# Splitting the last accumulator and its store, and holding one block's late products, in a two-layer attention and MLP kernel

## The chip, the cores and the metric

One core of one Trainium2 chip. The metric is device time in microseconds (us), the median of several executions. All executions compared here ran at a granted TensorE clock of 0.999 to 1.0. The experiments ran on two chips (e3, e4, e7 and e8 on one, the others on the other), so each median is set against runs of the kernel before in the same rounds.

## The reference

```python
# S = 2048 tokens, D = 1024, F = 3584, bfloat16; two identical rounds:
x = x + A(layernorm(x))   # sliding local attention: qkv, 8 taps at distance 2, softmax, output projection
x = x + B(layernorm(x))   # gate, up, relu(gate) * up, then W_down back to D columns
x = x + A(layernorm(x))
x = x + B(layernorm(x))
return x                  # 2048 x 1024, bfloat16
```

## The kernel before

The tokens are cut into 4 blocks of 512 (4 tiles of 128 rows each), and two rounds of 4 blocks make 8 steps, n = 0 to 7; below, "block 2" is the block of step 2, and so on. The steps are interleaved so that TensorE always has matmuls while VectorE does the attention of a later block. The residual x stays in SBUF in 16 tiles of 128x1024. Three parts matter.

The down projection of step n, and the store of a finished block:

```python
def down_steps(n, hold):
    ...
    def f_(half, s8):                      # half: 512 of the 1024 output columns; s8: a slab of 8 row blocks of W_down
        def f():
            if s8 == 0:
                accs[half] = [psum.tile([P, BLK], F32, tag="acc", ...)[:] for t in range(TPB)]   # 4 of 6 buffers
            ...
            for t in range(TPB):           # 4 token tiles
                with pe_group():
                    for jl in range(nfc):
                        mm(ac[t], lhsT=hT[:, j, t * P:(t + 1) * P], rhs=wsl[:, jl, :], ...)      # 128x512
            if s8 == NSL - 1:
                for t in range(TPB):
                    xs = xt[:, half * SLAB:(half + 1) * SLAB]
                    nc.vector.tensor_tensor(xs, ac[t], xs, op=ALU.add)     # "x add": PSUM + residual
        ...
    return [f_(half, s8) for half in range(2) for s8 in range(NSL)]

def store_x(n):                            # after the last step of a block: four stores of 128x1024
    for t in ...: sp_dma(out_dram[t * P:(t + 1) * P, :], x_tiles[t][:])
```

The attention logits of blocks 1 to 7 are sums of products on VectorE. A step makes the product `t` of head chunk c and then adds the previous one into `ac` (two halves h, 8 chunks each):

```python
def mult(h, c):
    def f():
        ...
        nc.vector.tensor_tensor(t[:], i0, i1, op=ALU.mult)     # n == 1: inside tc.issue_after(gate[0])
        if c > 1: add(h, c - 1)
        if c == KC - 1: add(h, c)

def add(h, c):
    nc.vector.tensor_tensor(o, ac[:], t[:], op=ALU.add)        # 128x2048, f32
```

VectorE's instruction order is made by a scheduler from the program; `tc.issue_after(ins)` adds an ordering edge, so that what is built inside it comes after `ins` on the same engine. `sp_dma` issues a DMA from the SP queue, always behind the DMA issued there before it. In the names of the profile, `dacc` is the accumulator of the down projection, `x` the residual, `t` and `ac` the products and their sum.

Of the kernel before, what the change touches and what calls it, by code (L numbers as in the profile page):

```python
# [8 lines left out]
F32 = mybir.dt.float32  # L9
ALU = mybir.AluOpType  # L10
# [3 lines left out]
P = 128  # L14
# [7 lines left out]
BLK = 512  # L22
TPB = BLK // P
EPS = 1e-5
NEG = -1.0e9
SLAB = 512
# [10 lines left out]
def kernel(  # L37
# [11 lines left out]
    nc = tc.nc  # L49
# [3 lines left out]
    NB = S // BLK  # L53
# [7 lines left out]
    NN = PAIRS * NB  # L61

    x_dram = A_x.flatten_outer_dims()
    out_dram = out.flatten_outer_dims()
# [16 lines left out]
    psum = ctx.enter_context(tc.tile_pool(name="psum", bufs=6, space=bass.MemoryType.PSUM))  # L81
# [28 lines left out]
    gate = [None]  # L110

    def sp_dma(dst, src, transpose=False):
        start = nc.sync.dma_start_transpose if transpose else nc.sync.dma_start
        if tail_sp[0] is None:
            tail_sp[0] = start(dst, src).ins
        else:
            with tc.issue_after(tail_sp[0]):
                tail_sp[0] = start(dst, src).ins

    @contextmanager  # L120
    def pe_group():
        if tail_pe[0] is None:
            yield
        else:
            with tc.issue_after(tail_pe[0]):
                yield

    def mm(*args, **kwargs):
        tail_pe[0] = nc.tensor.matmul(*args, **kwargs).ins  # L129

    def big_tile(shape, name, early=False):
        where = pool["early"] if early else big
        return where.tile(shape, BF16, tag="big", name=name)
# [27 lines left out]
    for t in range(NT):  # L161
        xt = xpool.tile([P, D], BF16, name=f"x{t}")
# [328 lines left out]
    def red_mm(n, prod, first, last):  # L491
        st = att[n]
        if first:
            st["L"] = psum_l.tile([P, W, P], F32, tag="L", name=f"L_{n}")
        with pe_group():
            for wh in range(2):
                for tq in range(TPB):
                    mm(st["L"][32 * tq:32 * tq + 32, WH * wh:WH * (wh + 1), :], lhsT=sel[:],
                       rhs=prod[:, WH * wh:WH * (wh + 1), tq * P:(tq + 1) * P],
                       start=first, stop=last, skip_group_check=True, tile_position=(0, 32 * tq))  # L500

    def qk_bcast(n, c, w0, nw):
        q, k = att[n][("q", c)], att[n][("k", c)]
        return _ap(q, 0, [[0, nw], [1, BLK]]), _ap(k, HALO - DIL * w0, [[-DIL, nw], [1, BLK]])
# [18 lines left out]
    def prod_sum_steps(n):  # L523
        st = att[n]

        def mult(h, c):
            def f():
                if h == 0 and c == 0:
                    st["s"] = big_tile([P, W, BLK], f"s_{n}")
                i0, i1 = qk_bcast(n, c, WH * h, WH)  # L530
                if c == 0:
                    t = work.tile([P, WH, BLK], F32, tag="ac", name=f"ac_{n}_{h}", bufs=1)
                    st["ac"] = t
                else:
                    t = work.tile([P, WH, BLK], F32, tag="t", name=f"t_{n}_{h}_{c}")
                    st[("t", c)] = t
                if n == 1:
                    with tc.issue_after(gate[0]):
                        nc.vector.tensor_tensor(t[:], i0, i1, op=ALU.mult)
                else:  # L540
                    nc.vector.tensor_tensor(t[:], i0, i1, op=ALU.mult)  # L541
                if c > 1:
                    add(h, c - 1)
                if c == KC - 1:
                    add(h, c)
            return f

        def add(h, c):
            ac, t = st["ac"], st.pop(("t", c))
            o = st["s"][:, WH * h:WH * (h + 1), :] if c == KC - 1 else ac[:]  # L550
            nc.vector.tensor_tensor(o, ac[:], t[:], op=ALU.add)  # L551

        def red():
            red_mm(n, st["s"], True, True)

        return [mult(h, c) for h in range(2) for c in range(KC)], red
# [97 lines left out]
    def gu_steps(n, ln):  # L654
        hold = {}

        def f_(j):
            def f():
                if j == 0:
                    hold["hT"] = pool["hid"].tile([P, FC, BLK], BF16, tag="hT", name=f"hT_{n}")  # L660
                s4, jl = j // 4, j % 4
                accs = {}
                for nm in ("g", "u"):
                    acc = psum.tile([P, BLK], F32, tag="acc", name=f"acc_{nm}")
                    with pe_group():
                        for kc in range(KC):
                            mm(acc[:], lhsT=slab[(nm, n, s4)][:, kc, jl * P:(jl + 1) * P], rhs=ln["xnT"][:, :, kc, :],
                               start=(kc == 0), stop=(kc == KC - 1))
                    accs[nm] = acc
                    if nm == "g":  # L670
                        r = pool["hid"].tile([P, BLK], BF16, tag="r", name="r", bufs=3)
                        tail_act[0] = nc.scalar.activation(r[:], acc[:], ACT.Relu).ins  # L672
                nc.vector.tensor_tensor(hold["hT"][:, j, :], accs["u"][:], r[:], op=ALU.mult)  # L673
            return f

        return [f_(j) for j in range(FC)], hold

    def down_steps(n, hold):
        b = n % NB
        accs = {}  # L680

        def f_(half, s8):
            def f():
                hT = hold["hT"]
                if s8 == 0:
                    accs[half] = [psum.tile([P, BLK], F32, tag="acc", name=f"dacc{t}")[:] for t in range(TPB)]
                ac = accs[half]
                nfc = min(8, FC - 8 * s8)
                wsl = slab[("d", n, half, s8)]
                for t in range(TPB):  # L690
                    with pe_group():
                        for jl in range(nfc):
                            j = 8 * s8 + jl
                            mm(ac[t], lhsT=hT[:, j, t * P:(t + 1) * P], rhs=wsl[:, jl, :],
                               start=(j == 0), stop=(j == FC - 1))
                if s8 == NSL - 1:
                    for t in range(TPB):
                        xt = x_tiles[b * TPB + t]
                        xs = xt[:, half * SLAB:(half + 1) * SLAB]
                        nc.vector.tensor_tensor(xs, ac[t], xs, op=ALU.add)  # L700
            return f

        return [f_(half, s8) for half in range(2) for s8 in range(NSL)]
# [106 lines left out]
    for n in range(NN):  # L810
        gu, hold = gu_steps(n, ln_b[n])
        want_gu(n, at, 2 * GRP)
        spread(gu, at, 2 * GRP)
        if n == 0:
            spread(pv_steps(1), at + 66.0, 5.5)
            ev.append((at + 105.0, store_o(1)))
            ev.append((at + 105.1, load_o(1)))
        elif n + 1 < NN:
            ev.append((at + 0.1, reds_n[n + 1]))
            ev.append((at + 0.2, lambda n=n: softmax(n + 1)))  # L820
            spread(pv_steps(n + 1), at + 12.0, 6.5)
            ev.append((at + 72.0, store_o(n + 1)))
            ev.append((at + 72.1, load_o(n + 1)))
        if n + 2 < NN:
            ln1(n + 2, at + 30.0, at + 58.0)
        at += 2 * GRP * FC
        if n + 2 < NN:
            want_qk(("qk", n + 2), at + 2 * GRP * KC)
            spread(qk_steps(n + 2, ln_a[n + 2], ("qk", n + 2)), at, GRP)
            sums, reds_n[n + 2] = prod_sum_steps(n + 2)  # L830
            spread(sums, at + GRP * (K_STEP[0] + 1.0), 4.4)
            at += 2 * GRP * KC
            if n + 2 >= NB:
                want_v(("v", n + 2), at + GRP * KC / 2, at + GRP * KC)
                spread(v_steps(n + 2, ln_a[n + 2], ("v", n + 2)), at, GRP)
                at += GRP * KC
                ev.append((at + 3.0, store_v(n + 2)))
        if n + 1 < NN:
            want_wo(n + 1, at + GRP * TPB, at + 2 * GRP * TPB)
            spread(wo_steps(n + 1), at, 2 * GRP)  # L840
            ln2(n + 1, [at + GRP * TPB + GRP * (t + 1) + 0.1 for t in range(TPB)], at + 2 * GRP * TPB + 31.0)
            at += 2 * GRP * TPB
        if n + 2 < NN:
            spread(load_v_steps(n + 2), at + 4.0, 6.5)
        want_down(n, at, GRP / 2)
        spread(down_steps(n, hold), at, 4 * GRP)
        at += GRP * FC
        if n >= NN - NB:
            ev.append((at + 4.0, store_x(n)))
    slab_events(ev)  # L850
    emit(ev)
# [32 lines left out]
```

## Time and profile before

| | before |
|---|---|
| median of 3 runs (range) | 1630.64 us (1630.27 to 1630.65) |
| span of the profiled run | 1628.4 us |
| TensorE (PE) busy | 1618.6 us, 99% |
| one wait of PE for VectorE (DVE) near 308 us | 0.76 us |
| last matmul's end to the end of the span | 3.90 us |

The page, first the busy line of each engine, then the chain that ended last as shares of the span:

```profile
span 1628.4 us, 18703 instructions
...
PE 1618.6 (99%) x7589; PEld 782.2 (48%) x7638; DVE 1062.6 (65%) x926; ACT 506.1 (31%) x1050; POOL 255.7 (16%) x220
...
PE 95%; DVE 4%; issue 1%; DMA 0%; POOL 0%; DVEq 0%
```

PE is the bound. The waits of PE (who waited for whom: us in total, times, longest) say what it ever waits for:

```profile
engine line waited for: us in total, times, longest us
PE scratch L129 <- DVE ones L296: 1.5, 1, 1.5
PE dacc L129 <- DVE x L700: 0.8, 1, 0.8
PE acc_v L129 <- DVE xnT_first L103: 0.6, 1, 0.6
PE tp L364 <- DVE xn_first L103: 0.4, 1, 0.4
```

All but the second are start-up. The second is in block 0's down projection. The timeline of PE there (start, length, what, and in brackets the idle time before it and what ended it):

```profile
299.65 7.72 PE L129 MATMUL dacc<-w_d,hT 128*128 128x512 bf16 x35
308.13 1.24 PE L129 MATMUL dacc<-w_d,hT 128*128 128x512 bf16 x5 [0.76 <-DVE x L700]
```

and that of DVE:

```profile
300.66 2.29 DVE L541 TENSOR_TENSOR t<-q,k 128x2048 f32<-128x2048 bf16 x1
302.87 2.28 DVE L551 TENSOR_TENSOR ac<-ac,t 128x2048 f32<-128x2048 f32 x1
305.18 2.29 DVE L541 TENSOR_TENSOR t<-q,k 128x2048 f32<-128x2048 bf16 x1
307.39 2.47 DVE L700 TENSOR_TENSOR x<-dacc,x 128x512 bf16<-128x512 f32 x4
309.79 2.28 DVE L551 TENSOR_TENSOR ac<-ac,t 128x2048 f32<-128x2048 f32 x1
```

The four accumulators of half 0 were complete near 303.9 us (estimate: PE ran dry at 307.37, 16 matmuls of 0.216 us later), but DVE was in the middle of its sums and came to the x adds only at 307.39. PE used the two free accumulators for half 1 and then had to wait for the first add.

The end of the kernel, in the timeline:

```profile
1595.81 28.65 PE L129 MATMUL dacc<-w_d,hT 128*128 128x512 bf16 x129
...
1622.63 2.92 SPq L118 DMA_DIRECT2D out_dram<-x  x4
...
1624.50 0.69 DVE L700 TENSOR_TENSOR x<-dacc,x 128x512 bf16<-128x512 f32 x1 [0.17 <-PE dacc L129]
1625.22 0.33 SPq L118 DMA_DIRECT2D out_dram<-x  x1
```

(The last line is the fourth of the four merged issues, from a narrower window.) The last matmul ends at 1595.81 + 28.65 = 1624.46, the last add at 1625.19, its store is issued at 1625.22, and the span ends at 1628.37. The table of stretches gives the traffic in that time; the last two columns are the busy share of the DMA engines and GB/s:

```profile
1625.20:1626.00 0.80, 0.00 (x0) 0.00 (x0) 0.00 (x0) 0.00 (x0) 0.00 (x0) 1.00 0.88 325
1626.00:1627.00 1.00, 0.00 (x0) 0.00 (x0) 0.00 (x0) 0.00 (x0) 0.00 (x0) 1.00 0.70 262
1627.00:1628.40 1.40, 0.00 (x0) 0.00 (x0) 0.00 (x0) 0.00 (x0) 0.00 (x0) 0.99 0.00 0
```

The DMA engines are nearly full until the data ends (at 1626.89 by the packets), then 1.48 us pass without data. From the DMA issues we can split them. The last figure of this line is the time from the issue of the last store to its landing (us), when its semaphore has all its increments:

```profile
out_dram<-x SPq DMA_DIRECT2D x1, 256.0 KB, 2.0
```

The landing comes 0.37 us after the last data, and the program then takes 1.10 us to end.

### The profile page before, as it was taken

How to read it: one execution, taken by the hardware profiler on the slowest of the kernel's cores; microseconds unless marked ns; L12 is line 12 of the kernel's file. 1: busy time of each engine (PE TensorE's matmuls, PEld its weight loads, DVE VectorE, ACT ScalarE, POOL GpSimd, SP SyncE). 2: the span in 40 equal slices, each digit the busy share in tenths (PEclk: the TensorE clock that was granted, in tenths of full speed). 3: DMA queues.
4: the chain of work that ended last, by engine and by line, in shares of the span. 5: the costliest groups of instructions: out<-in, count | busy, mean ns of one | idle time of the engine just before them, and what ended most of it. 6: DMA issues, size and time to landing. Idle time of an engine off the chain costs nothing.

```text
span 1628.4 us, 18703 instructions
## 1 busy us (share of the span) xinstructions
PE 1618.6 (99%) x7589; PEld 782.2 (48%) x7638; DVE 1062.6 (65%) x926; ACT 506.1 (31%) x1050; POOL 255.7 (16%) x220
## 2 busy tenths in 40 slices
PE   9999999999999999999999999999999999999999
PEld 6644445444544445444454444544445444444444
DVE  5799899985497927949179492894818958211211
ACT  4754313243241513405134051331513311131110
POOL 2421003310250102201052010520105100000000
PEclk9999999999999999999999999999999999999999
DMA  9579656746476485664857647577484764655451
GB/s 303 93 203 252 167 177 199 192 156 200 136 215 175 155 233 171 184 175 150 229 181 185 187 150 225 162 203 212 151 231 154 194 205 155 206 164 172 156 168 65
DMA packets 371463, 296.83 MB, mean 182 GB/s; under 512 B 142512, under 2 KB 351664, under 8 KB 370480
## 3 DMA queue, kind: packets, MB, share of 16 engines
q1 hardware_dynamic: 371088, 295.23, 63.2%
q8 instruction: 60, 0.98, 0.3%
q10 hardware_dynamic: 288, 0.39, 0.1%
q14 instruction: 27, 0.22, 0.0%
HBM read 256.77 MB, written 21.00 MB: 171 GB/s over the span
## 4 chain that ended last, share of the span: by engine, by line
PE 95%; DVE 4%; issue 1%; DMA 0%; POOL 0%; DVEq 0%
PE acc_g L129 24%; PE acc_u L129 24%; PE dacc L129 22%; PE acc_v L129 7%; PE acc_k L129 6%; PE acc_q L129 6%; PE acc_wo L129 6%; DVE t L541 2%; DVE ac L551 1%; PE L L129 1%; DVE pv L603 0%; DVE x L648 0%; DVE pv L604 0%; DVE ac L541 0%; DMA x<-in_A_x_dram 0%
## 5 line engine op out<-in xcount | busy, mean ns | idle before, releaser
L129 PE MATMUL acc_g<-xnT_b,w_g 128*128 128x512 bf16 x1792 | 423.4, 379 | 0.0
L129 PE MATMUL acc_u<-xnT_b,w_u 128*128 128x512 bf16 x1792 | 423.3, 379 | 0.0
L129 PE MATMUL dacc<-w_d,hT 128*128 128x512 bf16 x1759 | 386.5, 379 | 2.5 <-DVE x L700 0.8
L672 ACT ACTIVATE r<-acc_g 128x512 bf16<-128x512 f32 x224 | 133.4, 596 | 747.1 <-PE acc_g L129 746.0
L673 DVE TENSOR_TENSOR hT<-acc_u,r 128x512 bf16<-128x512 f32 x224 | 153.7, 687 | 315.1 <-PE acc_u L129 313.5
L129 PEld LDWEIGHTS <-hT 128*128 128x128 bf16 x1792 | 175.4, 98 | 212.3 <-issue 1.0
L129 PEld LDWEIGHTS <-w_g 128*128 128x128 bf16 x1792 | 174.8, 98 | 212.7 <-issue 3.0
L129 PEld LDWEIGHTS <-w_u 128*128 128x128 bf16 x1792 | 175.4, 98 | 211.4
L541 DVE TENSOR_TENSOR t<-q,k 128x2048 f32<-128x2048 bf16 x84 | 191.7, 2290 | 8.6 <-ACT k L480 5.8
L551 DVE TENSOR_TENSOR ac<-ac,t 128x2048 f32<-128x2048 f32 x84 | 191.7, 2282 | 0.4
L485 POOL COPY kh<-k 128x14 bf16<-128x14 bf16 x64 | 81.2, 1273 | 471.9 <-ACT k L480 471.8
L700 DVE TENSOR_TENSOR x<-dacc,x 128x512 bf16<-128x512 f32 x64 | 42.5, 687 | 164.0 <-PE dacc L129 164.0
L603 DVE TENSOR_TENSOR pv<-a,vhm 128x4096 bf16<-128x4096 bf16 x64 | 145.2, 2282 | 0.0
L129 PE MATMUL acc_wo<-w_o,oT 128*128 128x512 bf16 x496 | 111.0, 379 | 0.8
L245 POOL TENSOR_TENSOR st_b<-st_b,neg_half 128x1 f32<-128x1 f32 x29 | 56.4, 1956 | 288.6 <-ACT st_b L244 288.6
L245 POOL TENSOR_TENSOR st_a<-st_a,neg_half 128x1 f32<-128x1 f32 x32 | 41.9, 1315 | 319.2 <-ACT st_a L244 319.1
L484 POOL COPY k<-kh 128x14 bf16<-128x14 bf16 x48 | 70.5, 1469 | 65.9 <-DVE t L541 43.8
L129 PEld LDWEIGHTS <-oT 128*128 128x128 bf16 x512 | 50.0, 98 | 60.4
L604 DVE TENSOR_TENSOR pv<-pv 128x2048 bf16<-128x2048 bf16 x64 | 77.4, 1215 | 0.2
L476 ACT CAST q<-acc_q 128x512 bf16<-128x512 f32 x64 | 37.3, 583 | 73.2 <-PE acc_q L129 73.2
L240 ACT ACTIVATE xn_b<-x 128x1024 bf16<-128x1024 bf16 x29 | 30.3, 1045 | 89.3 <-DVE x L648 89.3
L480 ACT CAST k<-acc_k 128x512 bf16<-128x512 f32 x64 | 37.3, 583 | 63.0 <-PE acc_k L129 62.8
(131 smaller groups left out, 1209.1 us busy)
## 6 DMA issues: line engine op xcount, KB each, us to landing
w_g<-in_B_W_gate_dram SPq DMA_DIRECT2D x56, 1024.0 KB, 7.0
w_u<-in_B_W_up_dram SPq DMA_DIRECT2D x56, 1024.0 KB, 5.4
w_d<-in_B_W_down_dram SPq DMA_DIRECT2D x48, 1024.0 KB, 5.8
w_o<-in_A_wo_dram SPq DMA_DIRECT2D x16, 1024.0 KB, 7.2
vhm<-v_d SPq DMA_DIRECT2D x32, 284.0 KB, 6.9
v_d<-vT SPq DMA_DIRECT2D x8, 1024.0 KB, 10.0
oT<-o_d SPq DMA_DIRECT2D x32, 256.0 KB, 4.4
w_d<-in_B_W_down_dram SPq DMA_DIRECT2D x16, 512.0 KB, 4.0
```

What stands on the lines that cost most here:

```text
L129: tail_pe[0] = nc.tensor.matmul(*args, **kwargs).ins
L245: nc.gpsimd.tensor_tensor(rstd, vpe, neg_half[:, 0:1], op=ALU.pow)
L476: tail_act[0] = nc.scalar.copy(q[:], acc[:]).ins
L484: nc.gpsimd.tensor_copy(k[:, 0:HALO], khalo[n - 1][:, c, :])
L485: nc.gpsimd.tensor_copy(khalo[n][:, c, :], k[:, BLK:BLK + HALO])
L541: nc.vector.tensor_tensor(t[:], i0, i1, op=ALU.mult)
L551: nc.vector.tensor_tensor(o, ac[:], t[:], op=ALU.add)
L603: nc.vector.tensor_tensor(tt[:], a_bc, v_sh, op=ALU.mult)
L604: nc.vector.tensor_tensor(tt[:, 0:4], tt[:, 0:4], tt[:, 4:8], op=ALU.add)
L672: tail_act[0] = nc.scalar.activation(r[:], acc[:], ACT.Relu).ins
L673: nc.vector.tensor_tensor(hold["hT"][:, j, :], accs["u"][:], r[:], op=ALU.mult)
L700: nc.vector.tensor_tensor(xs, ac[t], xs, op=ALU.add)
```

## The change

The intent is twofold. The end is shortened: block 7 is stored in half rows as soon as each half is added, and the last tile's second half ends as two accumulators of 256 columns with an add and a store each. And block 2's products that come late are held behind the x adds of block 0's first half, so that PE need not wait for those.

```diff
-                if n == 1:
-                    with tc.issue_after(gate[0]):
+                behind = gate[0] if n == 1 else down_gate[0] if n == 2 else None
+                if behind is not None:
+                    with tc.issue_after(behind):
                         nc.vector.tensor_tensor(t[:], i0, i1, op=ALU.mult)
                 else:
                     nc.vector.tensor_tensor(t[:], i0, i1, op=ALU.mult)
...
+    down_gate = [None]
...
+                cols = [(t, 0, SLAB) for t in range(TPB)]
+                if n == NN - 1 and half == 1:
+                    cols[-1:] = [(TPB - 1, 0, SLAB // 2), (TPB - 1, SLAB // 2, SLAB)]
                 if s8 == 0:
-                    accs[half] = [psum.tile([P, BLK], F32, tag="acc", name=f"dacc{t}")[:] for t in range(TPB)]
+                    accs[half] = [psum.tile([P, BLK], F32, tag="acc", name=f"dacc{t}") for t, _, _ in cols]
...
-                for t in range(TPB):
+                for a, (t, c0, c1) in zip(ac, cols):
...
-                            mm(ac[t], lhsT=hT[:, j, t * P:(t + 1) * P], rhs=wsl[:, jl, :],
+                            mm(a[:, c0:c1], lhsT=hT[:, j, t * P:(t + 1) * P], rhs=wsl[:, jl, c0:c1],
...
-                        xs = xt[:, half * SLAB:(half + 1) * SLAB]
-                        nc.vector.tensor_tensor(xs, ac[t], xs, op=ALU.add)
+                        xs = xt[:, half * SLAB + c0:half * SLAB + c1]
+                        ins = nc.vector.tensor_tensor(xs, a[:, c0:c1], xs, op=ALU.add).ins
+                        if n == 0 and half == 0:
+                            down_gate[0] = ins
+                        if n == NN - 1:
+                            row = (b * TPB + t) * P
+                            col = half * SLAB + c0
+                            sp_dma(out_dram[row:row + P, col:col + c1 - c0], xs)
...
-        if n >= NN - NB:
+        if NN - NB <= n < NN - 1:
             ev.append((at + 4.0, store_x(n)))
```

The diff does not tell what the scheduler makes of the hold. The built program does. On DVE around block 0's first half (t5 stands for the product of chunk 5, and so on):

```
before:  ... t4, ac+=t3, t5,      x add x4,  ac+=t4, t6, ac+=t5, ...
after:   ... t4, ac+=t3, ac+=t4,  x add x4,  t5,     t6, ac+=t5, ...
```

More of the change, by code (lines that the diff above doesn't have):

```diff
@@ L693, in f @@
                             j = 8 * s8 + jl
-                            mm(ac[t], lhsT=hT[:, j, t * P:(t + 1) * P], rhs=wsl[:, jl, :],
+                            mm(a[:, c0:c1], lhsT=hT[:, j, t * P:(t + 1) * P], rhs=wsl[:, jl, c0:c1],
                                start=(j == 0), stop=(j == FC - 1))
                 if s8 == NSL - 1:
-                    for t in range(TPB):
+                    for a, (t, c0, c1) in zip(ac, cols):
                         xt = x_tiles[b * TPB + t]
-                        xs = xt[:, half * SLAB:(half + 1) * SLAB]
-                        nc.vector.tensor_tensor(xs, ac[t], xs, op=ALU.add)
+                        xs = xt[:, half * SLAB + c0:half * SLAB + c1]
[6 more added lines that the diff above has]
+                            sp_dma(out_dram[row:row + P, col:col + c1 - c0], xs)
             return f
```

## The prediction

> **What bounds the kernel now.** TensorE. The page has PE busy 1618.6 of 1628.4 us at full clock; the chain that ended last is 95% PE. The waits view of PE lists 3.3 us: start-up, and one wait of dacc for DVE (x add), 0.8 us. Otherwise only the end is exposed. Last matmul ends about 1624.48, last x add 1624.50 to 1625.19, its 256 KB store is issued about 1625.2, data moves until about 1626.8, the span ends at 1628.4 (timeline, stretches). The change can touch about 0.8 + 3.9 us (0.3%).
>
> **Part 1: sums of block 2 behind the adds.** In the timeline of block 0's down projection, PE runs dry at 307.37 and resumes at 308.13. Half 0 ended about 303.9 (estimate: 16 matmuls at 0.2157 us filled the two free accumulators), but DVE, which the Trainium skill ("TensorE: Matmul & The Clock Gate", specifications table) calls strict FIFO, reached the x adds only at 307.39, behind products and accumulations: the trace agrees with FIFO. The intent is to bring the adds forward. But in the changed kernel's instruction order only product t5 moves behind them; the accumulation of t4 takes its place. Before: ac(t3), t5, x adds, ac(t4). After: ac(t3), ac(t4), x adds, t5. A product takes 2.29 us, an accumulation 2.28 (timeline): the adds start at 307.4 to 307.5 as before, and the PE gap stays 0.75 to 0.87 us. No gain, 0.05 lost.
>
> **Part 2: the end.**
> - PE: 28 matmuls of 512 columns become 56 of 256. In block 0's v projection 56 of 256 columns with 16 of 512 took 9.57 us (15.12 to 24.69): 0.109 us each (estimate) against 0.2157 for 512. 56 x 0.109 - 28 x 0.2157 = +0.07 us. Weight loads (98 ns) still fit beneath; five accumulators fit the six buffers.
> - Last add: 0.69 us at 512 columns, about 0.40 at 256 (estimate from 0.69 and 2.28 us at 2048: 0.15 + 0.00104 per column). It ends about 0.5 instead of 0.71 us after the last matmul: -0.2 us. SP takes about 0.33 us per issue, so the last store goes out about 0.55 after: no more than -0.2.
> - Last store: 64 KB instead of 256. Its data took about 0.75 us (8 packets of 2 KB per engine, about 85 ns each). The skill ("DMA: Bandwidth & Descriptors", specifications) gives 512 B as the smallest size at line rate, just met here. Packets of 1 KB took 46 ns, of 256 B 18 ns, so 8 of about 27 ns: 0.2 to 0.3 us (estimate), -0.45 us. The 0.8 us from issue to data and the 1.6 us from last data to end stay.
> - The half-0 stores move to about 1598.5 to 1602, where DMA is idle. The last w_d slab goes out behind them near 1601.4, not 1596.9; needed about 1621.
>
> **Sum.** +0.05 + 0.07 - 0.2 - 0.45 = about -0.5 us: 1630.1 us, range 1629.5 to 1630.9, 8 in 10. Faster by over 2%: 0.003; within 2%: 0.994; slower: 0.003.
>
> **What would show it.** PE still waits 0.75 to 0.9 us for DVE x near 308; the last add takes about 0.4 us and ends 0.5 after the last matmul; from there to the end of the span 2.8 instead of 3.2 us.
>
> **What would make it wrong.** DVE reaching the adds early after all (0.8 us more gained); slower 256-column matmuls; stores queueing on SP; run spread (0.4 us in three runs).

## The result and the profile after

| | before | after |
|---|---|---|
| median (range), 4 runs each | 1630.45 us (1630.27 to 1630.65) | 1629.69 us (1629.53 to 1630.22) |
| PE's wait in block 0 | 0.76 us | 0.77 us |
| first matmul of block 0's down projection to the last matmul's end | 1344.88 us | 1344.97 us |
| last matmul's end to the end of the span | 3.90 us | 3.37 us |

The ratio is 0.9996 (95% interval 0.9979 to 1.0013): the same within 2%, and a gain of 0.76 us in the medians. A ratio is the mean time of one kernel's fast runs over that of the other's of the same rounds, so not quite the ratio of the medians quoted. In the means the difference is 0.67 us.

The two lower rows, summed, say 0.45 us. The profiled pair does not show what is left of the 0.67. Before block 0's down projection the two kernels do the same work, yet in twelve profiled executions of all kernels that point came between 279.56 and 280.10 us after the start, with no order to it (279.58 in the profile before, 279.72 after). So the rest is put down to noise, of the start-up above all; this is argued and not shown. This noise is also the reason why medians alone settle nothing here.

PE's waits after:

```profile
engine line waited for: us in total, times, longest us
PE scratch L129 <- DVE ones L296: 1.5, 1, 1.5
PE tp L364 <- DVE xn_first L103: 1.5, 2, 1.1
PE acc_v L129 <- DMA w_v<-in_A_wqkv_dram: 0.9, 1, 0.9
PE dacc L129 <- DVE x L706: 0.8, 1, 0.8
```

The wait for the x add is still there. DVE's timeline shows why:

```profile
300.81 2.29 DVE L542 TENSOR_TENSOR t<-q,k 128x2048 f32<-128x2048 bf16 x1
303.02 4.61 DVE L552 TENSOR_TENSOR ac<-ac,t 128x2048 f32<-128x2048 f32 x2
307.55 2.47 DVE L706 TENSOR_TENSOR x<-dacc,x 128x512 bf16<-128x512 f32 x4
309.94 4.48 DVE L540 TENSOR_TENSOR t<-q,k 128x2048 f32<-128x2048 bf16 x2
```

Two accumulations in a row now stand where an accumulation and a product stood; they take as long. From the start of the lone product to the x adds it is 307.55 - 300.81 = 6.74 us, before 307.39 - 300.66 = 6.73 us.

The end, in the timeline (the last three lines are from narrower windows):

```profile
1593.80 30.88 PE L129 MATMUL dacc<-w_d,hT 128*128 128x512 bf16 x167
...
1598.61 2.92 SPq L118 DMA_DIRECT2D out_dram<-x  x4
...
1622.84 3.04 SPq L118 DMA_DIRECT2D out_dram<-x  x5
...
1624.46 0.75 DVE L706 TENSOR_TENSOR x<-dacc,x 128x256 bf16<-128x256 f32 x2
1624.99 0.39 SPq L118 DMA_DIRECT2D out_dram<-x  x1
1625.47 0.40 SPq L118 DMA_DIRECT2D out_dram<-x  x1
```

The last add ends at 1624.46 + 0.75 = 1625.21, which is 0.52 us after the last matmul instead of 0.73. But the last store is issued at 1625.47, 0.26 us after its add, because SP is still issuing the store of the piece before. From the last matmul, that is 0.79 us; before the change it was 0.76. The traffic:

```profile
1625.20:1626.00 0.80, 0.00 (x0) 0.00 (x0) 0.00 (x1) 0.00 (x0) 0.00 (x0) 1.00 0.59 192
1626.00:1627.00 1.00, 0.00 (x0) 0.00 (x0) 0.00 (x0) 0.00 (x0) 0.00 (x0) 1.00 0.38 109
1627.00:1628.40 1.40, 0.00 (x0) 0.00 (x0) 0.00 (x0) 0.00 (x0) 0.00 (x0) 1.00 0.00 0
```

The DMA engines now have gaps: 0.59 and 0.38 busy instead of 0.88 and 0.70. By the packets, the last store's data runs from 1.69 to 2.04 us after the last matmul, instead of 1.60 to 2.43, and from there to the end it is 1.33 us instead of 1.48. The landing is not what became quicker:

```profile
out_dram<-x SPq DMA_DIRECT2D x1, 64.0 KB, 1.6
```

It follows the last data by 0.38 us, as before by 0.37. The program's end after the landing became shorter, 0.95 us instead of 1.10; the experiments show why.

### The profile page after: what moved, and what is told of

It is laid out like the page before. It is cut to its first block, busy times and chain, and to the rows that moved or that the text cites. A ratio compares the mean times of both kernels' runs of the same rounds, so it can differ in the third digit from the quotient of the medians.

```text
span 1628.1 us, 18770 instructions
## 1 busy us (share of the span) xinstructions
PE 1617.5 (99%) x7617; PEld 784.6 (48%) x7666; DVE 1062.6 (65%) x927; ACT 506.0 (31%) x1050; POOL 255.9 (16%) x220
## 4 chain that ended last, share of the span: by engine, by line
PE 95%; DVE 4%; issue 1%; DMA 0%; SPq 0%; DVEq 0%
PE acc_g L129 24%; PE acc_u L129 24%; PE dacc L129 22%; PE acc_v L129 7%; PE acc_k L129 6%; PE acc_q L129 6%; PE acc_wo L129 6%; DVE t L542 1%; DVE ac L552 1%; PE L L129 1%; DMA w_v<-in_A_wqkv_dram 0%; DVE pv L604 0%; DVE x L649 0%; DVE pv L605 0%; DVE ac L542 0%
## 5 line engine op out<-in xcount | busy, mean ns | idle before, releaser
L129 PE MATMUL dacc<-w_d,hT 128*128 128x512 bf16 (+1 forms) x1787 | 386.6, 376 | 2.5 <-DVE x L706 0.8
L542 DVE TENSOR_TENSOR t<-q,k 128x2048 f32<-128x2048 bf16 x81 | 184.8, 2290 | 8.5 <-ACT k L480 5.8
L706 DVE TENSOR_TENSOR x<-dacc,x 128x512 bf16<-128x512 f32 (+1 forms) x65 | 42.5, 679 | 164.0 <-PE dacc L129 164.0
```

Of the source, the lines that this page charges most:

```text
L129: tail_pe[0] = nc.tensor.matmul(*args, **kwargs).ins
L706: ins = nc.vector.tensor_tensor(xs, a[:, c0:c1], xs, op=ALU.add).ins
```

## The experiments

The theory at the start was that the end gives all of the gain, through the small last store, and that the hold gives nothing. Rival 1: the hold does what it was meant to do. Rival 2: in the end, what counts is that half of block 7's output left over 20 us earlier, not the size of the last store.

The table gives what the traces show, one profiled execution each. "Stretch" runs from the first matmul of block 0's down projection to the end of the last matmul, "tail" from there to the end of the span, "last issue" from the last matmul's end to the issue of the last store. Neither contains the start-up noise. "Landed" is the landing of the last store, again from the last matmul's end. (The profile models where a matmul ends; the sum of stretch and tail does not depend on it.) The last column but one is the median, the last one that of the kernel before in the same rounds.

| run | stretch | tail | last issue | landed | median | before |
|---|---|---|---|---|---|---|
| before | 1344.88 | 3.90 | 0.76 | 2.80 | | |
| after | 1344.97 | 3.37 | 0.79 | 2.42 | 1629.69 | 1630.45 |
| a0, after again | 1344.97 | 3.36 | 0.79 | 2.41 | 1629.68 | 1630.60 |
| e1, hold only | 1344.90 | 3.93 | 0.76 | 2.83 | 1630.38 | 1630.60 |
| e2, end only | 1344.97 | 3.35 | 0.79 | 2.41 | 1629.90 | 1630.60 |
| e3, half-row stores, no split | 1344.90 | 3.29 | 0.76 | 2.45 | 1629.84 | 1630.15 |
| e4, split, old stores | 1344.97 | 3.75 | 0.55 | 2.65 | 1630.46 | 1630.15 |
| e7, split, nothing stored early | 1344.97 | 3.73 | 0.82 | 2.71 | 1629.97 | 1630.15 |
| e5, sums really held | 1344.04 | 3.35 | 0.79 | 2.40 | 1628.85 | 1630.60 |
| e8, e5 with a second queue | 1344.04 | 3.06 | 0.54 | 2.11 | 1628.54 | 1630.15 |
| e9, e5 without the split | 1343.96 | 3.29 | 0.76 | 2.46 | 1628.58 | 1630.32 |
| e10, e5 with one last store | 1344.04 | 3.09 | 0.55 | 2.24 | 1628.56 | 1630.32 |

All outputs were correct.

The tail holds one part that no store's size sets. At the end of each program SP runs five instructions, one behind the other, that each wait for two DMA semaphores. Their order is the same in all twelve traces, and they start about 0.065 us apart when nothing holds them; 0.75 to 0.76 us of final steps follow. (The views leave these instructions out; this is from the records of the kept traces.) So the time from the landing to the end goes with the place of the last store's semaphore among the five: 1.10 us when it is in the first (before, e1, e4), 1.02 in the second (e7), 0.94 to 0.95 in the third (after, a0, e2, e5, e8), 0.84 to 0.85 in the fifth (e3, e9, e10). The place changed with the number of stores of block 7: 4, 5, 9 and 8 in these four groups. No run changed it alone. Ends of variants are therefore best compared by "landed". The same end profiled again agrees within 0.03 us in tail and landing.

### a0: the changed kernel again

No edit.

> Control, the changed kernel unedited. Theory (the tail did it, the hold did nothing) and rivals alike: about 0.7 us below before; one wait of dacc for DVE x of 0.7 to 0.85 us in block 0; last add's end to the end of the span 2.85 us (before: 3.18).

The median was 0.92 us below before, the mean 0.61; the wait and the tail came out as in the first run. The tail repeats to 0.01 us (between before and e1, which share their end, to 0.03) where the times do not repeat to 0.3.

### e1: only the hold

The changed kernel without its end:

```diff
-                if n == NN - 1 and half == 1:
-                    cols[-1:] = [(TPB - 1, 0, SLAB // 2), (TPB - 1, SLAB // 2, SLAB)]
...
-                        if n == NN - 1:
-                            ...  sp_dma(out_dram[row:row + P, col:col + c1 - c0], xs)
...
-        if NN - NB <= n < NN - 1:
+        if n >= NN - NB:
```

> Only the hold on block 2's products, end of the kernel as before. Theory: no gain; within 0.3 us of before (run spread), the wait of dacc for DVE x in block 0 stays 0.7 to 0.9 us, from the last add's end to the end of the span 3.2 us. Rival 1 (the intent: the hold lets PE go on): at least half of the 0.7 us gain shows here, and that wait is gone or under 0.3 us.

```profile
PE dacc L129 <- DVE x L704: 0.8, 1, 0.8
```

The wait of dacc for x stayed at 0.8 us, the tail at 3.93, and the mean of the runs is 0.04 us below before. The hold alone gives nothing; rival 1 falls.

### e2: only the end

```diff
-                behind = gate[0] if n == 1 else down_gate[0] if n == 2 else None
-                if behind is not None:
-                    with tc.issue_after(behind):
+                if n == 1:
+                    with tc.issue_after(gate[0]):
```

> The end as in the changed kernel, without the hold. Theory: all of the gain, as the changed kernel within 0.3 us, 0.5 to 0.8 us below before; last add's end to the end of the span 2.8 to 2.9 us; block 0's wait 0.76 us as before. Rival 1: less than half of the gain.

Tail 3.35 us, median 0.70 us below before: all of the gain.

### e5: hold the accumulations as well

If the held product's place was merely taken by an accumulation, holding that too must bring the x adds forward.

```diff
+            held = down_gate[0] if n == 2 else None
+            with (tc.issue_after(held) if held is not None else nullcontext()):
-            nc.vector.tensor_tensor(o, ac[:], t[:], op=ALU.add)
+                nc.vector.tensor_tensor(o, ac[:], t[:], op=ALU.add)
```

> The changed kernel with block 2's accumulations held behind the same adds as its products. Theory (the held product's place was taken by an accumulation of equal length): the four x adds start one DVE instruction earlier, at about 305.2 instead of 307.4 us; the 0.76 us wait of dacc disappears (under 0.1 us), and the time falls about 0.75 us below the changed kernel, 1.3 to 1.5 us below before. Rival (PE waits for something else there, or gives the time back later): the adds come earlier but the time stays within 0.3 us of the changed kernel.

DVE's timeline in this run:

```profile
300.90 2.29 DVE L542 TENSOR_TENSOR t<-q,k 128x2048 f32<-128x2048 bf16 x1
303.11 2.29 DVE L554 TENSOR_TENSOR ac<-ac,t 128x2048 f32<-128x2048 f32 x1
305.31 2.48 DVE L708 TENSOR_TENSOR x<-dacc,x 128x512 bf16<-128x512 f32 x4
307.70 2.29 DVE L540 TENSOR_TENSOR t<-q,k 128x2048 f32<-128x2048 bf16 x1
```

and PE's in the same place, without a break:

```profile
299.67 9.66 PE L129 MATMUL dacc<-w_d,hT 128*128 128x512 bf16 x44
```

The x adds start one instruction earlier, the wait is gone, and the time falls by 0.83 us against the changed kernel of the same rounds (1629.68 to 1628.85). The stretch falls by 0.93 us, more than the 0.77 us that the profile listed as wait. The reason is in how the wait is counted: it starts at the end of the last matmul, 0.38 us after its start, while matmuls start every 0.216 us when nothing stops them. The hole between starts was 1.15 us in the changed kernel, which is 0.93 above 0.216.

### e3: half-row stores without the split

e2 without the two lines that split `cols[-1:]`: one accumulator, one add and one store of 512 columns for the last tile as for the others.

```diff
-                if n == NN - 1 and half == 1:
-                    cols[-1:] = [(TPB - 1, 0, SLAB // 2), (TPB - 1, SLAB // 2, SLAB)]
```

> Stores of half rows, early for the first half, but one accumulator and one add of 512 columns for the last tile, no hold. Theory (only the last store's size counts): from the last matmul's end to the end of the span 3.40 to 3.60 us (before 3.90, changed kernel 3.37), last store issued 0.75 us after the last matmul as before; time 0.3 to 0.5 us below before. Rival 2 (the early stores' smaller backlog is the whole gain): 3.4 us or less, as the changed kernel.

The tail was 3.29 us: outside the theory's range, and shorter than with the split. The median is 0.31 us below before, where the trace says 0.60; one run of the five was a stray at 1631.51. The traffic in the last stretches:

```profile
1625.20:1626.00 0.80, 0.00 (x0) 0.00 (x0) 0.19 (x1) 0.00 (x0) 0.00 (x0) 1.00 0.48 164
1626.00:1627.00 1.00, 0.00 (x0) 0.00 (x0) 0.00 (x0) 0.00 (x0) 0.00 (x0) 1.00 0.39 131
1627.00:1627.90 0.90, 0.00 (x0) 0.00 (x0) 0.00 (x0) 0.00 (x0) 0.00 (x0) 0.63 0.00 0
```

and the issue of the last store, with its time to landing:

```profile
out_dram<-x SPq DMA_DIRECT2D x1, 128.0 KB, 1.7
```

The data of the last store, of 128 KB, lasted 0.51 us against 0.35 for the 64 KB of the changed kernel, and it landed 0.04 us later than in e2. The tail is shorter only because the program ends 0.84 us after the landing instead of 0.94 (e2) or 1.10 (before). With the 1.10 of the kernel before, the tail would have been 3.55 us, inside the theory's range. So e3 alone does not refute the theory. Nor did the early half make room in front of the last store here: its data starts 0.83 us after the issue, before the change 0.84. It is shorter (0.51 instead of 0.83 us) because half of its bytes have already gone.

### e4: the split without the stores

e2 with the old `store_x` for block 7: four stores of whole rows at the end.

```diff
-                        if n == NN - 1:
-                            ...  sp_dma(out_dram[row:row + P, col:col + c1 - c0], xs)
...
-        if NN - NB <= n < NN - 1:
+        if n >= NN - NB:
```

> Two accumulators and two adds of 256 columns for the last tile, but the four full-row stores at the end as before, no hold. Theory: the last store goes out about 0.54 us after the last matmul instead of 0.75 since nothing stands before it on the queue, its 256 KB take as long as before: 3.65 to 3.75 us from the last matmul to the end of the span (before 3.90); PE ends 0.07 us later; time 0.1 to 0.2 us below before, within run spread. If the split were what gains in the changed kernel, 3.4 us.

Tail 3.75 us, last issue at 0.55: as the theory had it. The shorter add brings the last issue 0.21 us forward if nothing stands before the last store on the queue, and is worth 0.15 us in the tail; the split matmuls take 0.07 to 0.09 us of it back. The median is 0.31 us above before, with a stray at 1632.06; the trace shows no cost that would explain it.

### e7: a small last store, but nothing stored early

e2, with tiles 0 to 2 stored as whole rows at the end, and tile 3 as 768 and 256 columns:

```diff
-                        if n == NN - 1:
+                        if n == NN - 1 and half == 1:
                             row = (b * TPB + t) * P
-                            col = half * SLAB + c0
-                            sp_dma(out_dram[row:row + P, col:col + c1 - c0], xs)
+                            col = 0 if c0 == 0 else SLAB + c0
+                            end = SLAB + c1
+                            sp_dma(out_dram[row:row + P, col:end], xt[:, col:end])
```

> As the changed kernel's end (no hold), but nothing is stored early: full rows for tiles 0 to 2, then 768 and 256 columns of tile 3 with a store each. Theory (last store's size): last matmul to end 3.35 to 3.55 us, time 0.4 to 0.7 us below before. Rival 2 (early stores are the gain): 3.7 us or more, within 0.2 us of before.

Tail 3.73 us and 0.18 us below before: rival 2's numbers. The last store is the same 64 KB as in the changed kernel, issued at 0.82 instead of 0.79, but its data ends 2.32 us after the last matmul instead of 2.04. The stretches show the queue of traffic before it:

```profile
1625.20:1626.00 0.80, 0.00 (x0) 0.00 (x0) 0.00 (x0) 0.00 (x0) 0.00 (x0) 1.00 0.91 339
1626.00:1627.00 1.00, 0.00 (x0) 0.00 (x0) 0.00 (x0) 0.00 (x0) 0.00 (x0) 1.00 0.76 254
```

The packets agree: those of the 192 KB piece in front move until 2.11 us, and the data of the last store starts 1.14 us after its issue instead of 0.90. So the theory holds only in part. The size of the last store counts (e3, and e10 against e8 below), but a small last store helps little while larger ones are still ahead of it. The half that left early does both: it makes the last store smaller, and it keeps the way free for the small one.

### e8: the next-to-last piece on another queue

Added to e5:

```diff
-                            sp_dma(out_dram[row:row + P, col:col + c1 - c0], xs)
+                            if c1 == SLAB // 2:
+                                nc.scalar.dma_start(out_dram[row:row + P, col:col + c1 - c0], xs)
+                            else:
+                                sp_dma(out_dram[row:row + P, col:col + c1 - c0], xs)
```

> The kernel with adds and products held (run e5), and the store of the last tile's next-to-last piece issued from ACT's queue instead of SP's. In the changed kernel the last store is issued 0.27 us after the last add's end, behind that piece's issue of 0.39 us. Theory (SP's queue ate what the shorter add gained): last store issued 0.02 to 0.05 us after the last add's end; last matmul to end about 3.15 us (3.35 in e5); time about 0.2 us below e5, 1628.6 us. Rival (DMA side sets it, not the queue): no change against e5, 3.3 us or more.

```profile
1623.76 0.41 DVE L708 TENSOR_TENSOR x<-dacc,x 128x256 bf16<-128x256 f32 x1
1623.87 0.35 ACTq L715 DMA_DIRECT2D out_dram<-x  x1
1624.20 0.33 SPq L118 DMA_DIRECT2D out_dram<-x  x1
```

The last store goes out 0.02 us after its add, at 0.54, and the tail is 3.06 us, 0.29 less than in e5. The Trainium skill ("DMA: Bandwidth & Descriptors", section "Issuing engines are not separate DMA queues") says that issuing from several engines saves only the sequencer's time to initiate a DMA; here that time is all that was wanted.

### e9 and e10: no split, or one store for both pieces

e9 is e5 without the split (the two lines taken out in e3). e10 is e5 with the split, but one store of 512 columns after the second add:

```diff
-                        if n == NN - 1:
+                        if n == NN - 1 and c1 == SLAB:
                             row = (b * TPB + t) * P
-                            col = half * SLAB + c0
-                            sp_dma(out_dram[row:row + P, col:col + c1 - c0], xs)
+                            col = half * SLAB
+                            sp_dma(out_dram[row:row + P, col:col + SLAB], xt[:, col:col + SLAB])
```

> Products and accumulations held (as run e5), half-row stores early, but one accumulator, one add and one store of 512 columns for the last tile. Theory (after e3: the early half-row stores are the whole gain of the end, splitting the accumulator costs): last matmul to end 3.29 us as in e3 (e5: 3.35), PE ends about 0.07 us earlier for the same start-up, time about 0.1 us below e5: 1628.7 us. Rival (the split gains): 3.4 us or more, slower than e5.

> As run e5 (products and accumulations held, two accumulators), but the last tile's two pieces leave with one store of 128 KB after the second add. Theory (SP's two issues ate the shorter add's gain): last store issued about 0.54 us after the last matmul instead of 0.79; last matmul to end about 3.1 us (e3's 3.29 less 0.21), close to e8's 3.06 without a second queue; time about 0.2 us below e5: 1628.6 us. Rival (the size of the last store decides): 3.35 us or more.

e9: tail 3.29 as in e3, stretch 0.07 us (unrounded) shorter than e5, together 0.12 us in the trace. But 0.11 us of this is the place of the last wait; counted to the landing, e5 and e9 agree to 0.02 us. The split with two stores on one queue gains nothing. e10: last issue at 0.55, tail 3.09 us:

```profile
1623.87 0.42 DVE L708 TENSOR_TENSOR x<-dacc,x 128x256 bf16<-128x256 f32 x1
1624.31 0.33 SPq L118 DMA_DIRECT2D out_dram<-x  x1
```

So the shorter add is worth its matmuls if only one store follows it. e8 against e10 is also nearly the size of the last store alone, with half 0 out early and the last issue at the same time (in e8 the other 64 KB go out just before, from ACT's queue): 64 KB land at 2.11 us, 128 KB at 2.24; the places of the last wait hide most of this in the tails. e8, e9 and e10 beat the kernel before by 1.6 to 1.8 us in the medians of the same rounds; among themselves they are within 0.04 us (1628.54, 1628.58, 1628.56, on two chip sessions), which is less than the run spread. By the traces (stretch and tail) e8 is 0.17 and e10 0.14 us ahead of e9.

## Why the prediction was right

The total was: 1630.1 us predicted with a range of 1629.5 to 1630.9, 1629.69 measured; -0.5 us predicted, -0.45 in the trace, -0.67 in the means, the rest put down to noise. That the total came so close is partly luck: the step of the last store's issue was 0.23 us too good, and 0.15 us of that came back through the program's end, which the prediction held constant. Point by point:

- **The hold gives nothing.** Right, and for the reason given. Predicted a wait of 0.75 to 0.87 us, measured 0.77; e1 shows no gain, e5 shows that the accumulation had taken the product's place. The instruction order of the built program was what made this readable before the run. DVE worked in that order, as the Trainium skill's row on queue depths says ("TensorE: Matmul & The Clock Gate", specifications table: strict FIFO) and as the twelve traces show: around these adds each has one of three orders, one for no hold, one for held products and one for held products and accumulations.
- **The matmuls of 256 columns.** Predicted +0.07 us from another place of the trace where such matmuls ran; the stretch rose by 0.07 (e2 against e3: no hold, with and without the split) to 0.09 us. The matmuls start every 0.109 us.
- **The last add.** Predicted to end about 0.5 us after the last matmul, measured 0.52; the add takes 0.41 us.
- **The last store's issue.** This step was wrong. The prediction expected the store about 0.55 us after the last matmul, -0.2 us. It went out at 0.79, 0.03 later than before. It had SP's time per issue, but mis-set the queue (it named "stores queueing on SP" only as a risk): the piece before is issued at 0.31 and not at 0.19, where its add ends, since SP is busy with tile 2's store until 0.21; its issue then takes 0.39 and not 0.33 us, and each issue leaves some 0.1 us until the next. e8 and e10 confirm it by taking the second issue away.
- **The last store's data.** Predicted -0.45 us, measured 0.83 to 0.35, so -0.48. The number was right and the size was the reason, as predicted; but of the -0.48, -0.32 come from half 0 alone, which leaves 128 KB for the last store (e3), and only the rest from the split. And the size works only with a free way: e7 keeps the 64 KB and loses two thirds of the tail's gain. The prediction had noted the early store of half 0 only as harmless. Its estimate of 27 ns for a packet of 512 B was met. The skill's smallest size at line rate, 512 B ("DMA: Bandwidth & Descriptors", "Specifications"), is not quite what the trace shows: packets of 512 B took 27 ns, of 1 KB 46 and of 2 KB 87, so they moved 19, 22 and 24 bytes per ns. The time from issue to data, predicted to stay, went from 0.84 to 0.90 us.
- **From the last data to the end.** Predicted to stay at 1.6 us; by the packets it was 1.48 and became 1.33. The landing did not change (0.37 and 0.38 us after the last data). The -0.15 us is the place of the last store's semaphore among the program's last waits, first before and third after. Nothing in the prediction was about it, and it makes up for most of the gain that the issue queue took.

What stays open: no run moves that place alone, so the differences of up to 0.26 us that it explains are read from twelve traces and not from an experiment of their own.

## What to carry to other kernels

Read the built instruction order before crediting an ordering edge: an edge that holds one instruction back lets the scheduler put another of the same length in its place, so hold everything that may stand in the way (here 0.93 us, from three more lines). At the end of a kernel, first get all early output off the queue early; splitting the last piece pays only if its stores do not queue behind each other on one issuing engine, so use one store or a second queue. Compare such ends at the landing of the last store: what followed it here, 0.84 to 1.10 us, went with the order of the program's last waits and not with the store. When an effect is smaller than the run spread, cut the trace at points that the change cannot move and compare the pieces.

## What the Trainium skill lacked or had wrong

- "TensorE: Matmul & The Clock Gate", section "Back-to-back issue gap", gives 131 ns per matmul of 512 columns as the sustained spacing in a stream of weight loads and matmuls, and calls N / 2.4 + 2.5 ns an isolated figure that over-counts there. Here, sustained over a whole kernel with a new weight load for each matmul, the spacing is 215.8 ns at 512 columns, and 109 ns where 256 columns follow each other; the "isolated" formula gives 215.8 and 109.2. (Another section of the page, "Wait — 56ns, not 53.3ns?", has 215.7 ns for back-to-back matmuls of 512.)
- "DMA: Bandwidth & Descriptors" calls the issue's cost "usually small relative to the DMA itself" and has, for an issue on SP or ACT before trn3, one figure without a method, 512 sequencer cycles (in its part on trn3 B0). Here a store of 128 partitions took SP 0.33 to 0.36 us to issue, and 0.39 to 0.41 when it came right behind another one, about 0.1 us after that one's end. It was not the number of columns: 256 took 0.39 to 0.40 behind another store and 0.33 in e8, and 768 behind another took 0.41 (e7). Two in a row cost the end of the kernel 0.25 us.
- The same page gives a DMA's fixed cost as about 2.0 us, fitted for another issuing path ("Anatomy of one DMA"). For the last stores here, issued from SP with the way free, the time from the issue to the landing, less that of the data, was 1.18 to 1.28 us: 0.83 to 0.90 before the first data and 0.35 to 0.40 after the last.
- No page says that a wait of PE counted from a matmul's end understates the hole: 0.77 us listed, 0.93 us gained when it was removed.
